# Three more tiles of the first batch in 16-bit pairs, and the work that turns weights into such pairs moved ahead of them

## The chip, the cores and the metric

The kernel runs on one core of one Trainium2 chip. The metric is the device time of one execution in microseconds (us); less is better. Besides TensorE (PE) the core has VectorE (DVE), ScalarE (ACT), GpSimd (POOL) and SyncE (SP), whose queue issues nearly all of the DMAs here.

## What is computed

Attention over channels, followed by a feed-forward layer on its result, in float32:

```python
qn = q / (np.linalg.norm(q, axis=1, keepdims=True) + 1e-06)      # q, k, v: (4, 6080, 256)
kn = k / (np.linalg.norm(k, axis=1, keepdims=True) + 1e-06)
s = kn.transpose(0, 2, 1) @ qn / tau                             # (4, 256, 256)
a = np.exp(s - s.max(-1, keepdims=True)); a /= a.sum(-1, keepdims=True) + 1e-09
x = (v @ a).reshape(24320, 256)
h = x @ w_in                                                     # 256 -> 2048
out = np.maximum(0.01 * h, h) @ w_out                            # 2048 -> 256
```

## The kernel before

The attention matrix of a batch is folded into the weights: W' = a @ w_in, so each batch needs only h = v @ W' and the second product. Every factor is held as a pair, a high part and a rest, and a product is made of three matmuls (high x high, rest x high, high x rest, `PASSES`). A pair is either of type fp32r or of 16 bits. 16-bit pairs need scales that are powers of two, found from the largest value of W_in (`w_scale`), of W_out (`wo_scale`) and of each tile of V (`v_scale`).

The tokens of a batch are cut into NT = 6 tiles of two halves, each half 512 columns wide in the first four tiles and 496 in the last two; tiles are counted here from 0 over the four batches, so tiles 0 to 5 are batch 0. The 2048 inner columns go in 8 pairs of blocks. One pair of one tile is a *window*; window w = 8 x tile + pair, 192 in all. `T16` is the first tile with 16-bit pairs: 6 before, that is all of batches 1 to 3.

A window of TensorE's list holds seven products (`block_product`, L811, 21 matmuls, a Strassen-like scheme) and, between them, the second product of the window before (`ffn_out`, L867, 24 matmuls). The seven products are collected through PSUM banks x and z. ACT copies bank x out (L847), DVE adds bank z to that (`add`, L841): add(h11), add(h22) and add(h12), in the order in which they come in a window. Bank z is used again only when its add is over, so a product that goes to z waits for DVE. From the sums, `leaky` makes pairs of the activated values: ACT the activation (L824), DVE the rest (L834, called g_split after what it writes).

All other work stands in slots between these: `slot` takes entries from a list for ACT, DVE or PE while their planned lengths fit the room of the slot (`put`, `put_steps`), and `at(w, ...)` enters work at the start of window w. The engines run their lists in this order. Such work is: the scores of the next batch (squares of q and k, added up on DVE, L223), sums of blocks of W_in for the products (`sums_work`, L999 to L1015), pairs of V (`v_split`, L762 to L773; `v_go` in 16 bits, `v_work` in fp32r), W_out's turning into 16-bit pairs (`wo_half`: DVE add L678, ACT, DVE L681, store), and copies of the output (`o_sb`) at the end of a tile.

A scale goes through four steps: `see` reduces a piece (DVE, L141), `gather` reduces these to one value per partition (L146) and stores it as a line in DRAM (0.5 KB, L147); `read`, a window later, fetches the line back into all partitions (64 KB into the tile `zeros`, L153); `find` makes the scale from it with five small DVE operations (L157 to L166), for V one more (L729). Before the change gather and find of a scale stand two windows or more apart.

## Time and profile before

| | |
|---|---|
| median of 3 runs | 2086.32 us (2085.83 to 2086.34) |
| the profiled execution | 2086.27 us, its span in the trace 2084.20 us |
| TensorE (PE) busy | 2076.7 us, 100% of the span, 9656 matmuls |
| VectorE (DVE) busy | 1600.7 us, 77%, 2905 instructions |
| ScalarE (ACT) busy | 1429.9 us, 69%, 2571 instructions |
| TensorE waiting for DVE's add before a product to bank z | 1.4 us in all, 3 times |

TensorE is occupied from end to end and granted its full clock throughout. The time is therefore the length of TensorE's list, and every wait that enters it. DVE and ACT have idle time on the average; how much there is in one window, and in which part of it, is seen only in the timeline.

### The profile page before, as it was taken

The numbers are of one execution on the slowest core, as the hardware profiler recorded it, in microseconds if no ns is written. First come the engines' busy times: TensorE is split into PE (matmuls) and PEld (weight loads), VectorE is DVE, ScalarE is ACT, GpSimd is POOL, SyncE is SP. The second block draws the span as 40 slices with busy tenths as digits, with TensorE's granted clock in tenths as the row PEclk, the third lists the DMA queues.
The fourth block names the chain that finished last, engine by engine and source line by source line (L and its number), as shares of the span: only waits on it lengthen the run. The fifth ranks groups of instructions, "written<-read, shape, count | busy, mean of one in ns | idle before, by whom it ended". The sixth has DMA issues, their size and how long they took to land.

```text
...
## 1 busy us (share of the span) xinstructions
PE 2076.7 (100%) x9656; PEld 1213.5 (58%) x9656; DVE 1600.7 (77%) x2905; ACT 1429.9 (69%) x2571; POOL 3.3 (0%) x11
## 2 busy tenths in 40 slices
...
GB/s 361 397 167 206 201 244 212 171 180 180 185 136 130 106 104 99 104 105 96 175 111 131 115 106 117 104 106 75 120 154 106 83 84 75 66 86 73 66 73 29
DMA packets 120168, 283.47 MB, mean 136 GB/s; under 512 B 15072, under 2 KB 40160, under 8 KB 120032
## 3 DMA queue, kind: packets, MB, share of 16 engines
...
HBM read 227.93 MB, written 53.75 MB: 135 GB/s over the span
## 4 chain that ended last, share of the span: by engine, by line
PE 98%; DVE 1%; DMA 1%; ACT 0%; issue 0%; SPq 0%; ACTq 0%; DVEq 0%
PE ps_o L867 48%; PE ps_x L811 24%; PE ps_z L811 16%; PE ps_s L253 3%; PE ps_y L811 2%; PE ps_y L253 2%; PE ps_s L1060 1%; PE ps_o L253 1%; DMA qk_raw<-in_k_dram 1%; PE ps_y L558 0%; PE ps_y L1060 0%; DVE sq_acc L210 0%; PE ps_z L558 0%; SPq L201 0%; ACT sq L209 0%
## 5 line engine op out<-in xcount | busy, mean ns | idle before, releaser
L867 PE MATMUL ps_o<-g_split,w_out_split 128*128 128x512 f16 (+3 forms) x4608 | 1123.3, 380 | 0.0
L834 DVE TENSOR_TENSOR g_split<-g,g_split 128x512 f16<-128x512 f32 (+3 forms) x768 | 525.0, 684 | 208.3 <-ACT g_split L824 201.1
L811 PE MATMUL ps_x<-v_split,w_split 128*128 128x512 f16 (+3 forms) x2280 | 620.3, 381 | 0.1
L867 PEld LDWEIGHTS <-w_out_split 128*128 128x128 f16 x3456 | 338.2, 98 | 400.0
L824 ACT ACTIVATE g<-h 128x512 f32<-128x512 f32 (+1 forms) x576 | 360.4, 626 | 281.7 <-DVE h L841 279.0
L841 DVE TENSOR_TENSOR h<-ps_z,h 128x512 f32<-128x512 f32 (+1 forms) x520 | 354.7, 682 | 234.0 <-ACT h L847 225.9
L847 ACT COPY h<-ps_x 128x512 f32<-128x512 f32 (+1 forms) x576 | 331.5, 575 | 292.8 <-PE ps_x L811 291.6
L811 PEld LDWEIGHTS <-w_split 128*128 128x128 f16 x3024 | 288.8, 98 | 342.2 <-issue 11.9
L811 PE MATMUL ps_z<-v_split,w_split 128*128 128x512 f16 (+3 forms) x1560 | 423.0, 380 | 1.4 <-DVE h L841 1.4
L824 ACT ACTIVATE g_split<-h 128x512 f16<-128x512 f32 (+3 forms) x576 | 351.4, 610 | 0.0
L867 PEld LDWEIGHTS ps_o<-g_split,w_out_split 128*128 128x128 f32 x1152 | 216.4, 188 | 43.5
L830 ACT CAST g_split<-g 128x512 f16<-128x512 f32 (+3 forms) x192 | 118.0, 615 | 5.9
L811 PEld LDWEIGHTS ps_x<-v_split,w_split 128*128 128x128 f32 x576 | 107.7, 188 | 22.4 <-ACT h L847 0.4
L824 ACT ACTIVATE g<-ps_x 128x512 f32<-128x512 f32 (+1 forms) x192 | 113.1, 589 | 9.7 <-PE ps_x L811 7.4
L764 DVE SCALAR_TENSOR_TENSOR v_split<-v_raw,v_scale,v_split 128x512 f16<-128x512 f32 (+1 forms) x125 | 93.2, 745 | 4.4
L223 DVE TENSOR_TENSOR sq_acc<-sq_acc,sq 128x512 f32<-128x512 f32 x141 | 96.3, 683 | 0.2
L220 ACT ACTIVATE sq<-qk_raw 128x512 f32<-128x512 f32 x141 | 87.5, 630 | 0.0
L811 PEld LDWEIGHTS ps_z<-v_split,w_split 128*128 128x128 f32 x408 | 76.2, 188 | 16.7 <-DVE h L841 1.4
L253 PE MATMUL ps_s<-qk_split 128*128 128x512 f32 x192 | 73.2, 391 | 0.0
L232 DVE TENSOR_TENSOR qk_split<-qk_raw,qk_split 128x512 fp32r<-128x512 f32 x96 | 65.6, 683 | 0.0
L785 DVE TENSOR_TENSOR v_raw<-v_raw 128x512 f32<-128x512 f32 (+1 forms) x94 | 64.0, 681 | 1.4
L253 PE MATMUL ps_y<-qk_split 128*128 128x512 f32 x192 | 60.3, 336 | 0.0
...
## 6 DMA issues: line engine op xcount, KB each, us to landing
w_split<-w_dram SPq DMA_DIRECT2D x144, 448.0 KB, 3.8
...
```

What stands on the lines that cost most here:

```text
L220: return nc.scalar.activation(out=out, in_=self.chunk(j), func=AF.Square)
L223: return nc.vector.tensor_tensor(out=self.acc[0], in0=self.acc[0], in1=sq, op=ALU.add)
L232: return nc.vector.tensor_tensor(out=sp[:, :, 1, :], in0=self.chunk(j), in1=f32(sp[:, :, 0, :]), op=ALU.subtract)
L253: mm = nc.tensor.matmul(out=out, lhsT=lhsT, rhs=rhs, start=start, stop=stop, skip_group_check=True)
L764: return nc.vector.scalar_tensor_tensor(out=sp[:, 1, 0:w], in0=src, scalar=up, in1=sp[:, 0, 0:w], op0=ALU.mult, op1=ALU.subtract)
L811: mm = nc.tensor.matmul(out=ps[:, 0:n], lhsT=w[:, x, a, :], rhs=sp[:, y, 0:n], start=first and k == 0, stop=k == 2, skip_group_check=True,)
L824: return nc.scalar.activation(out=to, in_=h[:, 0:n], func=AF.Prelu, alpha=0.01, scale=G_SCALE if i >= T16 else 1.0)
L830: issued["act"] = nc.scalar.copy(out=sp[:, 0, 0:n], in_=out[:, 0:n])
L834: issued["dve"] = nc.vector.tensor_tensor(out=sp[:, 1, 0:n], in0=out[:, 0:n], in1=f32(sp[:, 0, 0:n]), op=ALU.subtract)
L841: issued["dve"] = nc.vector.tensor_tensor(out=h[:, 0:n], in0=ps[:, 0:n], in1=h[:, 0:n], op=ALU.add)
L847: issued["act"] = nc.scalar.copy(out=h[:, 0:n], in_=ps[:, 0:n])
L867: issued["pe"] = nc.tensor.matmul(out=o_ps[i][j][h][:, 0:n], lhsT=wo_lhsT(i, x, f, h), rhs=sp[:, y, 0:n], start=p == 0 and early and k == ...
```

## The change

`T16` becomes 3, so tiles 3, 4 and 5 of batch 0 (w24 to w47) use 16-bit pairs too. All that these need is moved ahead of them:

- `w16_work(p)` in window 16 + p turns W' of one pair into 16 bits: at the window's start two DVE adds of 128x448 (high + rest), then in slots ACT, DVE, ACT, DVE, and a store of 448 KB. Tiles 3 to 5 load that (448 KB a window instead of 896).
- `wo_half`, eight times, now runs from w13 on (before: w24 to w34), and the loads of the result (`wo_load`) come in tile 2 instead of tile 5.
- The scales of W_in and W_out are found from sums that ACT accumulates (`summed`: squares for W_in, absolute values for W_out) instead of 16 DVE reduces. `gather` has one more small operation and `find(True)` five more (`roots`). W_in's gather is put in at w7 and its find at w9, W_out's at w10 and w12.
- Tiles 3 to 5 get their pairs of V by `v_scale_work` and `v_go`: gather, read, find, and then the 16-bit pair.
- The squares of batch 1 begin at w10 instead of w8, their loads are held back, the sums of W_in (`sums_work`) are chained one behind the other.
- `slot` no longer takes the list in its order, but by the window by which an entry is wanted (`wanted`, `due`).

The diff, cut to what the sections below speak of:

```diff
-    T16 = NT
+    T16 = 3
...
         def gather(self):
             last = nc.vector.tensor_reduce(out=self.top, in_=self.most, axis=AX.X, op=ALU.max)
+            last = nc.vector.tensor_scalar(
+                out=self.top, in0=self.top, scalar1=2.0**126, scalar2=None, op0=ALU.min
+            )
             nc.sync.dma_start(out=self.line, in_=self.top)
             at(now[0] + 1, self.read)
             return last
 
         def read(self):
...
+    def w16_work(p):
+
+        w, n = w_split[T16 - 1, p], NS * P // 2
+        o = work.tile([P, 2, NS * P], F16, name="w16", tag="qk_split", bufs=3)
+        t = [temp(name="w_whole")[:, 0:n] for _ in range(2)]
+        hi, lo = (f32(w[:, x].rearrange("p s f -> p (s f)")) for x in range(2))
+        xs = [slice(x * n, (x + 1) * n) for x in range(2)]
+        for x in range(2):
+            run("dve", lambda: nc.vector.tensor_tensor(out=t[x], in0=hi[:, xs[x]], in1=lo[:, xs[x]], op=ALU.add))
+
+        def high(x):
+            return nc.scalar.activation(out=o[:, 0, xs[x]], in_=t[x], func=AF.Copy, scale=w_scale.up)
+
+        def low(x):
+            ins = nc.vector.scalar_tensor_tensor(
+                out=o[:, 1, xs[x]], in0=t[x], scalar=w_scale.up, in1=o[:, 0, xs[x]], op0=ALU.mult, op1=ALU.subtract
+            )
+            if x:
+                nc.sync.dma_start(
+                    out=w16_dram[p].rearrange("p x f -> p (x f)"), in_=o.rearrange("p x f -> p (x f)")
+                )
+                w16_done[p] = now[0]
+            return ins
+
+        put_steps([
+            ("act", 0.6, lambda: high(0)), ("dve", 0.7, lambda: low(0)),
+            ("act", 0.6, lambda: high(1)), ("dve", 0.7, lambda: low(1)),
...
+        w, src = w_tile(i), w_dram[i // NT, p]
+        if T16 <= i < NT:
+            assert p in w16_done
+            src = w16_dram[p]
+        nc.sync.dma_start(out=f32(w.rearrange("p x s f -> p (x s f)")), in_=src.rearrange("p x f -> p (x f)"))
         w_split[i, p] = w
...
     def slot(queue, room):
         engine = queue.split("_")[0]
-        while todo[queue] and todo[queue][0][0] <= room and todo[queue][0][1].ready():
-            length, fn = todo[queue].popleft()
+        while True:
+            order = sorted(range(len(todo[queue])), key=lambda n: todo[queue][n][1].due or now[0] + 3)
+            for n in order:
+                length, fn = todo[queue][n]
+                if fn.ready() and (length <= room or fn.due is None):
+                    break
+            else:
+                return
+            if length > room:
+                return
+            del todo[queue][n]
             room -= length
             with in_order(engine):
...
             else:
-                at(w + 1, v_scale_work, i + 1)
-                at(w + 3, v_go, i + 1, 3)
-                at(w + 4, v_go, i + 1, 3)
-                at(w + 5, v_go, i + 1, 3)
-                at(w + 6, v_go, i + 1, 3)
+                with wanted(w + 2 if i < NT - 1 else None):
+                    at(w + 1, v_scale_work, i + 1)
+                with wanted(w + 6 if i < NT - 1 else None):
+                    for x in (3, 4, 5, 6):
...
-        begin_at, span = (NPAIR, 20) if b == 1 else (0, 28)
+        begin_at, span = (NPAIR + 2, 19) if b == 1 else (0, 28)
         when = {j: w0 + begin_at + j * span // NCHUNK for j in range(NCHUNK)}
         for i in range(len(sc.groups)):
-            at(max(w0 - 2, when[i * G] - (1 if b == 1 else 3)), lambda sc=sc, i=i: sc.load(i, qk_raw()))
+            if b == 1:
+                at(when[i * G] - 1, raw_wanted.append, (sc, i))
+            else:
+                at(max(w0 - 2, when[i * G] - 3), lambda sc=sc, i=i: sc.load(i, qk_raw()))
...
+    def wo_go(n):
+        if n < wo_n:
+            with wanted(TL + n - 3):
+                put_steps([*wo_half(n), ("call", wo_go, n + 1)], True)
+
+    TL = (T16 - 1) * NPAIR
+    with wanted(NPAIR + 2):
+        for n in range(wo_n):
+            at(NPAIR + n // 4, put, "act", 0.65, lambda n=n: summed(
+                f32(wo_region(n)), wo_scale.most[:, n:n + 1], AF.Abs
+            ))
+    at(NPAIR - 1, put, "dve", 0.2, w_scale.gather)
+    at(NPAIR + 1, put, "dve", 1.2, lambda: w_scale.find(True), (), True)
+    at(NPAIR + 2, put, "dve", 0.2, wo_scale.gather)
+    at(NPAIR + 4, put, "dve", 0.6, wo_scale.find, [("dve", 0.3, weights_down), ("call", wo_go, 0)], True)
+    for p in range(NPAIR):
+        with wanted(TL + p):
+            at(TL + p, w16_work, p)
```

`order`'s rows show where this puts work on DVE. L901, L908 and L251 are the lines of L834, L841 and L223 after the change; a name ahead of `<-` is what a row writes, and `[waits ...]` are the semaphores that it waits for (DMAHW is a DMA).

**W_in's scale, w8 and w9.** On DVE, before, from add(h11) of w9 (h_1810) over add(h22) (h_1851) to add(h12):

```order
L841 TENSOR_TENSOR h_1810<-ps_z_1805,h_1810 128x512 [waits PE_49,Activation_49]
L223 TENSOR_TENSOR sq_acc_1695<-sq_acc_1695,sq_1815 128x512 [waits DVE_49,Activation_49]
L834 TENSOR_TENSOR g_split_1829<-g_1828,g_split_1829 128x512 [waits Activation_49]
L841 TENSOR_TENSOR h_1851<-ps_z_1806,h_1851 128x512 [waits DMAHW0_49,Activation_49]
L223 TENSOR_TENSOR sq_acc_1695<-sq_acc_1695,sq_1838 128x512 [waits DVE_49]
L834 TENSOR_TENSOR g_split_1864<-g_1863,g_split_1864 128x512 [waits PE_49,Activation_49]
L841 TENSOR_TENSOR h_1836<-ps_z_1806,h_1836 128x512 [waits PE_49]
```

The same place after the change, from the row behind add(h11) on; L165 to L176 are the find, and h_1880 is add(h22):

```order
L165 TENSOR_REDUCE w_scale_134<-zeros_72 128x1 [waits DMAHW6_49]
L184 TENSOR_SCALAR w_scale_134<-w_scale_134 128x1 [waits DVE_49]
L187 TENSOR_SCALAR w_scale_134<-w_scale_134 128x1 [waits DVE_49]
L190 TENSOR_SCALAR w_scale_134<-w_scale_134 128x1 [waits DVE_49]
L191 TENSOR_SCALAR w_scale_134<-w_scale_134 128x1 [waits DVE_49]
L192 ISA w_scale_134<-w_scale_134 128x2 [waits DVE_49]
L168 TENSOR_SCALAR w_scale_134<-w_scale_134 128x1 [waits DVE_49]
L169 TENSOR_SCALAR w_scale_134<-w_scale_134 128x1 [waits DVE_49]
L172 TENSOR_SCALAR w_scale_134<-w_scale_134 128x1 [waits DVE_49]
L176 TENSOR_SCALAR w_scale_134<-w_scale_134 128x1
L901 TENSOR_TENSOR g_split_1856<-g_1855,g_split_1856 128x512 [waits Activation_49]
L908 TENSOR_TENSOR h_1880<-ps_z_1824,h_1880 128x512 [waits DMAHW0_49,Activation_49]
```

The gather of this scale (L148, L149) stands in w8 right behind add(h11) and one v_split step. The ten rows of find, with a wait for the read, came between add(h11) and the pair that follows it; two additions of squares went.

**V's scale for tile 4, w26 and w27.** On DVE, before, from add(h11) of w27 (h_3617) to its add(h22):

```order
L841 TENSOR_TENSOR h_3617<-ps_z_3612,h_3617 128x512 [waits PE_49,Activation_49]
L223 TENSOR_TENSOR sq_acc_1695<-sq_acc_1695,sq_3549 128x512 [waits DVE_49]
L834 TENSOR_TENSOR g_split_3632<-g_3631,g_split_3632 128x512 [waits Activation_49]
L681 SCALAR_TENSOR_TENSOR wo16_3423<-wo_whole_3422,wo_scale_128,wo16_3423 128x512
L223 TENSOR_TENSOR sq_acc_1695<-sq_acc_1695,sq_3595 128x512 [waits DVE_49]
L1006 TENSOR_TENSOR win_s_3526<-win_s_3526,win_s_3113 128x512
L841 TENSOR_TENSOR h_3659<-ps_z_3613,h_3659 128x512 [waits Activation_49]
```

After the change, in w26 from the last reduce of the scale to add(h22), with its gather (L148, L149):

```order
L143 TENSOR_REDUCE v_scale_3544<-v_raw_3391 128x1
L148 TENSOR_REDUCE v_scale_3544<-v_scale_3544 128x1 [waits DVE_49]
L149 TENSOR_SCALAR v_scale_3544<-v_scale_3544 128x1 [waits DVE_49]
L1106 TENSOR_TENSOR win_t_3438<-win_s_2358,win_t_3438 128x512
L908 TENSOR_TENSOR h_3678<-ps_z_3625,h_3678 128x512 [waits Activation_49]
```

and in w27 from the row behind add(h11) to add(h22) (h_3786):

```order
L251 TENSOR_TENSOR sq_acc_1923<-sq_acc_1923,sq_3739 128x512 [waits DVE_49,Activation_49]
L1097 TENSOR_TENSOR win_s_2360<-win_s_2360,win_s_2358 128x512
L901 TENSOR_TENSOR g_split_3750<-g_3749,g_split_3750 128x512 [waits Activation_49]
L165 TENSOR_REDUCE v_scale_3544<-zeros_72 128x1 [waits DMAHW5_49]
L168 TENSOR_SCALAR v_scale_3544<-v_scale_3544 128x1 [waits DVE_49]
L169 TENSOR_SCALAR v_scale_3544<-v_scale_3544 128x1 [waits DVE_49]
L172 TENSOR_SCALAR v_scale_3544<-v_scale_3544 128x1 [waits DVE_49]
L176 TENSOR_SCALAR v_scale_3544<-v_scale_3544 128x1
L796 TENSOR_SCALAR v_scale_3544<-v_scale_3544,rest_down_146 128x1 [waits DVE_49]
L829 TENSOR_SCALAR v_split_3760<-v_raw_3391,v_scale_3544 128x496
L831 SCALAR_TENSOR_TENSOR v_split_3760<-v_raw_3391,v_scale_3544,v_split_3760 128x496 [waits DVE_49]
L908 TENSOR_TENSOR h_3786<-ps_z_3730,h_3786 128x512 [waits Activation_49]
```

The find (L165 to L176 and L796) and the first half step of v_split (L829, L831) came ahead of add(h22), one window behind the gather; before, the pair of V needed no scale and conversions of W_out stood here.

**The start of a window of tile 2 (w18).** On DVE, before, from the last but one pair of w17 to the add(h11) of w18 (h_2706) and the v_split step behind it:

```order
L834 TENSOR_TENSOR g_split_2680<-g_2679,g_split_2680 128x512 [waits Activation_49]
L834 TENSOR_TENSOR g_split_2685<-g_2684,g_split_2685 128x512 [waits Activation_49]
L841 TENSOR_TENSOR h_2706<-ps_z_2701,h_2706 128x512 [waits PE_49,Activation_49]
L769 CAST v_split_2714<-v_raw_2482 128x512 [waits DMAHW2_49]
L773 TENSOR_TENSOR v_split_2714<-v_raw_2482,v_split_2714 128x512 [waits DVE_49]
```

After the change, at the start of w18, whose add(h11) is h_2763:

```order
L901 TENSOR_TENSOR g_split_2732<-g_2731,g_split_2732 128x512 [waits Activation_49]
L251 TENSOR_TENSOR sq_acc_1923<-sq_acc_1923,sq_2736 128x512 [waits DVE_49,Activation_49]
L901 TENSOR_TENSOR g_split_2740<-g_2739,g_split_2740 128x512 [waits Activation_49]
L595 TENSOR_TENSOR w_whole_2753<-w_split_2428 128x448
L595 TENSOR_TENSOR w_whole_2754<-w_split_2428 128x448
L908 TENSOR_TENSOR h_2763<-ps_z_2758,h_2763 128x512 [waits DMAHW4_49,PE_49,Activation_49]
L251 TENSOR_TENSOR sq_acc_1923<-sq_acc_1923,sq_2768 128x512 [waits DVE_49,Activation_49]
```

The two adds of W' (L595) came between the last pair of the window before and add(h11).

## Rows read from the trace of the kernel before

**Rows 1.** The page: busy time and instructions by engine; the chain that ended last.
```profile
PE 2076.7 (100%) x9656; PEld 1213.5 (58%) x9656; DVE 1600.7 (77%) x2905; ACT 1429.9 (69%) x2571; POOL 3.3 (0%) x11
...
PE 98%; DVE 1%; DMA 1%; ACT 0%; issue 0%; SPq 0%; ACTq 0%; DVEq 0%
```

**Rows 2.** Timeline of PE, one fp32r window (w20): start, us, operation, count.
```profile
301.43 0.84 PE L811 MATMUL ps_x<-v_split,w_split 128*128 128x512 f32 x3
...
304.60 0.84 PE L811 MATMUL ps_z<-v_split,w_split 128*128 128x512 f32 x3
...
309.59 0.84 PE L811 MATMUL ps_z<-v_split,w_split 128*128 128x512 f32 x3
...
311.63 0.84 PE L811 MATMUL ps_x<-v_split,w_split 128*128 128x512 f32 x3
```

**Rows 3.** Timeline of PE, one 16-bit window (tile 19): first products of two windows.
```profile
1700.91 0.81 PE L811 MATMUL ps_x<-v_split,w_split 128*128 128x512 f16 x3
...
1710.62 0.81 PE L811 MATMUL ps_x<-v_split,w_split 128*128 128x512 f16 x3
```

**Rows 4.** Tiles by stretch: length; PE, PEld, DVE, ACT, POOL; PEclk, DMA share, GB/s.
```profile
260.60:342.20 81.60, 81.60 (x361) 67.54 (x360) 71.89 (x117) 62.83 (x113) 0.00 (x0) 1.00 0.64 220
...
425.30:510.90 85.60, 85.60 (x387) 71.76 (x387) 66.04 (x129) 55.57 (x102) 0.00 (x0) 1.00 0.51 171
510.90:596.10 85.20, 85.20 (x383) 71.46 (x382) 67.00 (x135) 51.97 (x95) 0.00 (x0) 1.00 0.58 192
...
942.30:1024.60 82.30, 81.66 (x390) 39.61 (x389) 62.67 (x125) 53.56 (x102) 0.00 (x0) 1.00 0.39 124
1024.60:1104.90 80.30, 80.30 (x382) 38.63 (x381) 67.08 (x140) 50.80 (x96) 0.00 (x0) 1.00 0.46 146
```

**Rows 5.** Timeline of DVE in w80: add(h22).
```profile
950.63 0.66 DVE L841 TENSOR_TENSOR h<-ps_z,h 128x496 f32<-128x496 f32 x1
```

**Rows 6.** Timeline of PE in w80: the product behind that add [idle time, releaser].
```profile
951.35 0.79 PE L811 MATMUL ps_z<-v_split,w_split 128*128 128x496 f16 x3 [0.60 <-DVE h L841]
```

**Rows 7.** Timeline of DVE, tile 2: around add(h11) in w17, add(h11) in w22.
```profile
272.50 0.68 DVE L834 TENSOR_TENSOR g_split<-g,g_split 128x512 fp32r<-128x512 f32 x1
273.10 0.68 DVE L841 TENSOR_TENSOR h<-ps_z,h 128x512 f32<-128x512 f32 x1
...
323.46 0.69 DVE L841 TENSOR_TENSOR h<-ps_z,h 128x512 f32<-128x512 f32 x1 [0.18 <-PE ps_z L811]
```

**Rows 8.** DMA issues by line: KB each and median us from issue to landing.
```profile
v_scale_line<-v_scale SPq DMA_DIRECT2D x18, 0.5 KB, 7.5
...
w_scale_line<-w_scale SPq DMA_DIRECT2D x1, 0.5 KB, 9.9
```

**Rows 9.** Tiles v_scale_line (stores and reads) and zeros (reads): landing times.
```profile
DMA to landing us min/median/max: 4.4/6.6/8.2
...
DMA to landing us min/median/max: 4.4/5.4/6.2
```

**Rows 10.** Timeline of DVE in w8: the v_split step behind add(h11).
```profile
181.90 0.68 DVE L773 TENSOR_TENSOR v_split<-v_raw,v_split 128x512 fp32r<-128x512 f32 x1
```

**Rows 11.** Timeline of DVE in w41, v_scale's find: first, last, and the v_split behind.
```profile
546.64 0.28 DVE L157 TENSOR_REDUCE v_scale<-zeros 128x1 f32<-128x128 f32 x1
...
547.57 0.21 DVE L729 TENSOR_SCALAR v_scale<-v_scale,rest_down 128x1 f32<-128x1 f32 x1
...
549.10 0.48 DVE L762 TENSOR_SCALAR v_split<-v_raw,v_scale 128x512 f16<-128x512 f32 x1
```

**Rows 12.** Timeline of SP's DMA queue in w8.
```profile
182.60 0.81 SPq L750 DMA_DIRECT2D v_raw<-in_vT_dram  x2
```

**Rows 13.** Timeline of PE: the first product of w9.
```profile
189.21 0.84 PE L811 MATMUL ps_x<-v_split,w_split 128*128 128x512 f32 x3
```

**Rows 14.** DVE groups by form: SCALAR_TENSOR_TENSOR to 16 bits, 256 and 512 columns.
```profile
L602 DVE SCALAR_TENSOR_TENSOR w_rest<-w_s,w_scale,w_rest 128x256 f16<-128x256 f32 x48 | 21.0, 478 | 0.0
...
L681 DVE SCALAR_TENSOR_TENSOR wo<-wo_whole,wo_scale,wo 128x512 f16<-128x512 f32 x8 | 6.0, 745 | 0.0
```

141 lines of the change are left out of this document (92 added, 49 removed).

## The prediction

> **What bounds the kernel now.** I read the page's busy shares and chain first, then busy time by tile, then the timelines of single windows (a window is one pair of one tile; w = 8 x tile + pair, tiles counted from 0, so the change's tiles 4 to 6 are numbers 3 to 5, w24 to w47). TensorE is busy all the time: the chain that ended last is 98% PE, while DVE has 77% of the span and ACT 69% [rows 1]. So a change pays only where it shortens TensorE's own list, and costs only where it makes TensorE wait, which it hardly does now.
>
> How long TensorE takes depends on the pair's type. An fp32r window starts at 301.43 and the next at 311.63: 10.20 us [rows 2]. A 16-bit window of the same 45 matmuls takes 9.71 (1700.91 to 1710.62) [rows 3]. The 496-wide tiles of batch 0 (tiles 4 and 5, from 425.3 and 510.9) take 85.6 and 85.2; their counterparts in batch 1 (tiles 10 and 11, from 942.3 and 1024.6), already 16-bit with the same extra matmuls, 82.3 and 80.3 [rows 4].
>
> The second thing to see is how tight the other engines' dates are. The products of a window that go through bank z start 3.17 us (304.60) and 8.16 us (309.59) after its first matmul [rows 2]; each needs a DVE add that empties the bank (add(h11) and add(h22)). Where that add is late, TensorE waits at once: in w80 an o_sb copy stands ahead of add(h22), the add ends at 950.63 + 0.66 = 951.29, and the product starts at 951.35, after 0.60 of idling [rows 5, 6]. So an add has to end 0.05 us before its product: at +3.12 and +8.11 in an fp32r window, and at +7.7 for the second one in a 16-bit window (8.16 x 9.71 / 10.20, less 0.05). Now add(h11) of an ordinary tile-2 window is over at +2.3 (w22 begins at 321.83; 323.46 + 0.69), 0.8 us early [rows 7].
>
> **What the change gives.** Tile 3: eight windows by 10.20 - 9.71 = 3.9 us (a half window is lost at its start, where the second product still has the tile before's fp32r pairs, and another won in w48). Tiles 4 and 5: 85.6 + 85.2 - 82.3 - 80.3 = 8.2 us [rows 4]; w80's stall is in the 82.3, and w32 of the changed kernel has the same order. TensorE's instruction counts do not change. Together **-12.1 us**, if TensorE never waits.
>
> **What it costs.** Four kinds of work come to other engines; three meet TensorE's dates.
>
> *A, the scale of W_in.* A scale is found by a gather on DVE, a 0.5 KB store, a 64 KB broadcast read and a find on DVE. The store takes 7.5 (v_scale) to 9.9 us (w_scale) to land, the read 5.4, from 4.4 to 6.2 in 20 of them [rows 8, 9]. Now find stands two windows behind the gather and waits for nothing. In the change the gather is in w8 behind the v_split that ends at 181.90 + 0.68 = 182.58, so over at 182.9 (two ops of at most 0.2) [rows 10, 11]; its store queues behind SP's two 512 KB loads (182.60, 0.81 long) and goes at 183.4 [rows 12]. Data: 183.4 + 8.7 (half way between 7.5 and 9.9) + 5.4 = 197.5. Find stands second in w9, which begins at 189.21 [rows 13], ahead of add(h22): it would start at +8.3, when add(h22) should be over. Behind the data come ten small ops (the six now from 546.64 to 547.57 + 0.21 = 1.1 [rows 11]; five of them without the last one 0.9, and five more for the roots: 1.8), one g_split start to start (0.60) and the add (0.68), so it ends at 8.3 + 3.1 = 11.4 against 8.1: **+3.3**. Bounds: store 7.5 and read 4.4 give 183.4 + 11.9 + 3.1 - 189.2 - 8.1 = 1.1; 9.9 and 6.2 give 5.3.
>
> *B, the scale of tile 4's V.* In w26 the gather comes behind add(h11) (ends +2.3), two square sums, a g_split, and one reduce: 2.3 + 4 x 0.62 + 0.3 = +5.1. With 0.2 to the issue, 7.5 and 5.4 the data are there at w26 + 18.2, which is w27 + 8.5, since w26 is 9.71 long. In w27 find's six ops (1.1), the first half of v_split (0.48 [rows 11] and an STT of 0.745 [rows 14], about 1.1 from start to start) and the add (0.68) come behind it: add(h22) ends at 11.4 against 7.7, **+3.7**. Bounds: 2.6 with a read of 4.4, 5.3 with 8.2 and 6.2, the longest V scale transfers [rows 9]. The same pair for tile 3 (w18 to w20) and tile 5 (w33 to w35) is two windows apart and costs nothing, as now; the wo scale (w10 to w13) too.
>
> *C, tile 2.* W' of tile 3 to 5 is turned into 16-bit pairs in w16 to w23: per window two adds and two STT on DVE of 128x448. 512 columns take 0.69 and 0.745, 256 STT columns 0.478 [rows 7, 14]; by that slope 448 take about 0.62 and 0.68, and start to start 0.54 and 0.60, since an instruction that does not need the one before starts 0.08 before its end (272.50 and 273.10, each 0.68 long [rows 7]). The two adds stand right ahead of add(h11): 1.08 of the 0.8 us that it has. Then it is over at about +3.1 in the ordinary window, on the date to 0.05: between 0 and 0.25 us late in each, and 0.5 where DVE came late out of the window before; I take 1.7 in all. In w17, whose start holds the o_sb copies, add(h11) ends at 273.78 now, w17 + 3.0 (260.6 + 10.2 = 270.8 [rows 4, 7]), and then at 4.1: +1.0. In all, DVE's list of tile 2 (from 260.6) is now 117 instructions [rows 4], 77 us by their lengths, 69 start to start. By the order the change adds 14 adds, 14 STT, 9 wo conversion steps, 8 v_split and 4 reduce steps and some small ones of V's scale (34 us of lengths), and takes 9 reduces, 9 win sums, 12 v_split steps and 2 square sums away (20): 91 by lengths, 81 start to start, in 81.6 us of TensorE [rows 4]. It is uneven: counted by the same prices, w20 and w21 hold 11.3 and 10.7 for 10.20, so 1.6 more. C: **+4.3**; bounds 1.0 (w17 alone, all else covered) and 7.
>
> *The rest costs nothing.* ACT gets 16 casts and 16 accumulating passes, about 8 us in tile 2, whose 62.8 busy of 81.6 [rows 4] hide them; without that cover each late copy would cost what a DVE add does. SP gets eight 448 KB stores in tile 2, where DMA is at 0.64 of its time [rows 4]; W' reloads for tiles 3 to 5 are halved. The 16 reduces that go are on DVE, which is not the bound where they stood.
>
> Sum: -12.1 + 3.3 + 3.7 + 4.3 = -0.8. The profiled execution took 2086.27 for a span of 2084.20, and the median of the runs is 2086.32, so 2085.5: no change that 0.2% (4.2 us, about what a measurement of this kernel can tell) would show.
>
> **The rivals.** *The waits are mostly covered (faster).* If the round trips are at their short end (A 1.1, B 2.6) and DVE's overlap leaves only w17's late add (C 1.0), the sum is -12.1 + 4.7 = -7.4: 2078.9; with nothing waiting at all 2074.2. For it: the short ends do occur, and 0.05 us in one add per window decides six windows of C. Against: both landings are medians over 18 transfers [rows 8], and w8's store goes behind two large loads. The Trainium skill, page "DMA: Bandwidth & Descriptors", section "Anatomy of one DMA", puts the fixed cost of a transfer (there one of GpSimd's queue) near 2.0 us: by that page the round trip would be about 4 us as an estimate, A and B would vanish and the time be 2085.5 - 7.0 = 2078.5. The rows (7.5 and 5.4) do not agree with it in this kernel, so it gets no weight beyond the short end's.
>
> *DVE becomes the bound of tile 2 (slower).* If the 0.08 us of overlap is not had by instructions that wait for ACT or a DMA, the list counts by its lengths: 91 for 81.6 us, so C is 9.4, and -12.1 + 7.0 + 9.4 = +4.3, 2090.6; with tile 3 (about 81 of lengths in 79) 2092. It decides once C passes 9.3, that is when nearly nothing of 117 overlaps is left. For it: nearly every added instruction waits on another engine. Against it: 272.50 to 273.10 holds for a g_split that waits for ACT. On a page: the Trainium skill, "VectorE: DVE Perf Modes", section "The DRAIN you can't avoid", says that the next op does not start until the pipe is empty, and by it lengths add up in full; the trace disagrees with the 0.60 between starts of 0.68 [rows 7].
>
> That the 16-bit windows are not shorter in batch 0 I give no weight: 144 windows already run so.
>
> **How the numbers follow.** Forecast (waits of 8 to 16 us, 2082.1 to 2090.5): 0.60. Waits covered, below 2082.1: 0.28. DVE the bound, or both round trips at their long ends (5.3 + 5.3 + 5.5 = +4.0 net) above 2090.5: 0.12. These are also same, faster and slower. Range 2079 to 2091: it leaves out about 0.1 of the first rival (below its own sum) and 0.1 of the second.
>
> **What would show it.** In the changed profile: 16-bit windows of 9.71 and 9.41 in w24 to w47; one stall of TensorE on add(h22) of 3.3 in w9 with DVE's find waiting for the zeros read, and one of 3.7 in w27; tile 2 at 85.9 instead of 81.6, w17, w20 and w21 longest. I am wrong if find does not wait (round trip under 10 us), if tile 2 stays under 83, or if tile 3 to 5 do not come down.

## The result, and the profile after

| | before | after |
|---|---|---|
| median | 2086.33 us (2085.83 to 2086.84) | 2106.94 us (2105.91 to 2110.58, 4 runs) |
| ratio, 95% interval | | 1.0102 [1.0084, 1.0119] |
| profiled execution, span | 2086.27, 2084.2 us | 2105.91, 2104.1 us |

The changed kernel is slower by 20.6 us, outside the range of 2079 to 2091. The page of the changed kernel, busy time by engine and the chain that ended last (before: [rows 1]):

```profile
PE 2075.0 (99%) x9656; PEld 1116.9 (53%) x9656; DVE 1621.2 (77%) x2982; ACT 1442.2 (69%) x2619; POOL 3.3 (0%) x11
...
PE 91%; DMA 3%; DVE 3%; ACT 3%; issue 1%; SPq 0%; DVEq 0%; ACTq 0%
```

TensorE is busy for 1.7 us less than before, but the chain is no longer its own: DMA, DVE and ACT hold 9% of it. The same by tiles 1 to 5 (stretch, length, then busy time of PE, PEld, DVE, ACT, POOL; PEclk, DMA share, GB/s):

```profile
179.20:272.80 93.60, 85.64 (x362) 69.14 (x361) 66.61 (x123) 66.47 (x128) 0.00 (x0) 0.96 0.48 173
272.80:365.90 93.10, 85.50 (x362) 66.14 (x361) 83.01 (x143) 67.94 (x126) 0.00 (x0) 1.00 0.61 199
365.90:453.00 87.10, 81.39 (x369) 38.36 (x369) 75.18 (x142) 61.91 (x115) 0.52 (x1) 0.96 0.65 178
453.00:535.40 82.40, 81.77 (x391) 39.64 (x390) 67.91 (x135) 55.63 (x106) 0.00 (x0) 1.00 0.50 162
535.40:615.70 80.30, 80.30 (x383) 38.57 (x382) 67.25 (x141) 50.89 (x95) 0.00 (x0) 1.00 0.49 146
```

Tiles 4 and 5 took 85.6 and 85.2 before [rows 4] and now take what their counterparts in batch 1 take. Tile 2 took 81.6 and takes 93.1. Tile 1, for which 3.3 more were forecast, took 11.4 more, and tile 3 lost in one window twice what it gained in the others. Here and below the length of a window is the distance of its first product from that of the next window, read from PE's timeline as in [rows 2, 3]; the two of w9, for instance, are 189.99 and 208.28. All these lengths and waits are read from one profiled execution of each kernel. Four places make the loss:

| place | before | after | difference |
|---|---|---|---|
| w9 | 10.20 | 18.29 | +8.1 |
| w12 | 10.20 | 13.33 | +3.1 |
| tile 2 (w16 to w23) | 81.6 | 93.1 | +11.5 |
| w27 | 10.20 | 17.32 | +7.6 over 9.71, the 16-bit window's length |
| tile 3 without that, tiles 4 and 5 | 253.8 | 242.2 | -11.6 |
| all else | | | +1.2 |

**w9**, four engines of the timeline: SP's queue, ACT's copy of bank x, DVE's find and add(h22), and the product that waits (start, us, operation; in brackets idle time before it and who ended it):

```profile
184.27 0.38 SPq L152 DMA_DIRECT2D w_scale_line<-w_scale  x1
193.43 0.33 SPq L160 DMA_DIRECT2D zeros<-w_scale_line  x1
...
194.32 3.80 SPq L961 DMA_DIRECT2D out_dram<-o_sb  x4
...
202.36 0.58 ACT L914 COPY h<-ps_x 128x512 f32<-128x512 f32 x1 [6.05 <-DMA out_dram<-o_sb]
...
199.50 0.28 DVE L165 TENSOR_REDUCE w_scale<-zeros 128x1 f32<-128x128 f32 x1 [6.08 <-DMA zeros<-w_scale_line]
...
202.98 0.69 DVE L908 TENSOR_TENSOR h<-ps_z,h 128x512 f32<-128x512 f32 x1 [1.03 <-ACT h L914]
...
203.00 1.65 PE L878 MATMUL ps_x<-v_split,w_split 128*128 128x512 f32 x3 [4.93 <-ACT h L914]
```

There are two waits side by side. DVE's find waits 6.1 us for its data, as step A said. But TensorE waits for ACT: the copy needs a buffer that an o_sb tile still holds (ACT's copies `h`, the o_sb tiles, the scratch that ACT's sums write to and the halves of W' and W_out take turns in one ring of nine buffers), and the store of that tile left late, because the read of the scale's line stood at the head of SP's queue until its line had landed (184.27 to 193.4, 9.1 us). The four stores behind it went at 194.3 to 198.1.

The same place in one-microsecond slices (columns as above):

```profile
200.00:201.00 1.00, 0.00 (x0) 0.00 (x0) 0.82 (x6) 0.00 (x0) 0.00 (x0) 1.00 0.97 393
201.00:202.00 1.00, 0.00 (x0) 0.00 (x0) 0.92 (x4) 0.00 (x0) 0.00 (x0) 0.84 1.02 392
202.00:203.00 1.00, 0.00 (x0) 0.00 (x1) 0.02 (x1) 0.58 (x1) 0.00 (x0) 0.50 0.89 340
...
207.00:208.00 1.00, 1.00 (x4) 0.80 (x3) 0.38 (x2) 0.84 (x2) 0.00 (x0) 0.50 0.64 158
208.00:209.00 1.00, 1.00 (x5) 0.82 (x4) 0.56 (x1) 0.00 (x0) 0.00 (x0) 0.75 1.03 430
209.00:210.00 1.00, 1.00 (x6) 0.80 (x5) 0.00 (x0) 0.72 (x2) 0.00 (x0) 1.00 0.67 280
```

TensorE has stood since 198.1. In the slice from 201 its granted clock falls to 0.50, the lower of its two levels (1.2 GHz), and stays there until the slice from 208. So w9 loses 4.9 us of its 8.1 by standing and 2.6 by the restart at the lower clock: from 203.00 to the window's end at 208.28 it takes 5.28 us for what a plain window does in 2.72. The other 0.6 us are short waits ahead of the long one.

**w12.** SP's queue and ACT:

```profile
213.99 0.33 SPq L152 DMA_DIRECT2D wo_scale_line<-wo_scale  x1
221.63 0.33 SPq L160 DMA_DIRECT2D zeros<-wo_scale_line  x1
...
224.06 1.36 SPq L229 DMA_DIRECT2D qk_raw<-in_q_dram  x1
...
226.72 0.42 SPq L229 DMA_DIRECT2D qk_raw<-in_k_dram  x1
...
234.57 0.63 ACT L248 ACTIVATE sq<-qk_raw 128x512 f32<-128x512 f32 x1 [4.28 <-DMA qk_raw<-in_k_dram]
```

Four q and k loads go in one bunch behind the read of W_out's line and two W_in loads; ACT's square of that data waits, and its next copy of bank x stands behind the square (TensorE idle 2.79 us).

**w27.** SP's store and read of tile 4's V scale, DVE's find and add(h22), the product behind it:

```profile
392.43 0.38 SPq L152 DMA_DIRECT2D v_scale_line<-v_scale  x1
...
401.96 0.32 SPq L160 DMA_DIRECT2D zeros<-v_scale_line  x1
...
406.69 0.29 DVE L165 TENSOR_REDUCE v_scale<-zeros 128x1 f32<-128x128 f32 x1 [6.12 <-DMA zeros<-v_scale_line]
...
408.92 0.69 DVE L908 TENSOR_TENSOR h<-ps_z,h 128x512 f32<-128x512 f32 x1
...
409.66 1.44 PE L878 MATMUL ps_z<-v_split,w_split 128*128 128x512 f16 x3 [5.66 <-DVE h L908]
```

This is step B's chain, longer: w27 begins at 396.06, the find at +10.6 (forecast +8.5), and the restart is again at the lower clock (0.50 in the slices from 408 to 412).

**Tile 2.** Groups of DVE and then of PE by line (busy us, mean ns, idle us before them and who ended it):

```profile
L901 DVE TENSOR_TENSOR g_split<-g,g_split 128x512 fp32r<-128x512 f32 x33 | 22.7, 689 | 3.5 <-ACT g_split L891 3.3
L908 DVE TENSOR_TENSOR h<-ps_z,h 128x512 f32<-128x512 f32 x24 | 16.4, 685 | 5.2 <-ACT h L914 5.1
L251 DVE TENSOR_TENSOR sq_acc<-sq_acc,sq 128x512 f32<-128x512 f32 x17 | 11.6, 685 | 0.1
L595 DVE TENSOR_TENSOR w_whole<-w_split 128x448 f32<-128x448 f32 x16 | 9.3, 620 | 0.9 <-DMA wo_dram<-wo 0.9
L601 DVE SCALAR_TENSOR_TENSOR w<-w_whole,w_scale,w 128x448 f16<-128x448 f32 x13 | 8.6, 678 | 0.0
...
L878 PE MATMUL ps_x<-v_split,w_split 128*128 128x512 f32 (+1 forms) x97 | 27.9, 394 | 1.8 <-ACT h L914 1.8
L878 PE MATMUL ps_z<-v_split,w_split 128*128 128x512 f32 x72 | 21.5, 407 | 5.8 <-DVE h L908 5.6
```

DVE is occupied 83.0 us (before 71.9, [rows 4]), which alone is more than the 81.6 us that TensorE needs, and TensorE waits for its adds in nearly every window: 5.6 us for DVE and 1.8 for ACT. The other 4 us show as busy time (85.5 us for the work of 81.6, at a granted clock of 1.00). The place is the product to bank z behind add(h11), the one of the first add in a window. In w17, which begins at 283.06:

```profile
283.06 0.84 PE L878 MATMUL ps_x<-v_split,w_split 128*128 128x512 f32 x3
...
285.69 0.96 PE L878 MATMUL ps_x<-v_split,w_split 128*128 128x512 f32 x3
...
287.62 0.96 PE L878 MATMUL ps_z<-v_split,w_split 128*128 128x512 f32 x3 [0.96 <-DVE h L908]
```

It starts 4.56 us into the window where a plain one has 3.17 [rows 2], 1.4 us late, of which the profile shows 0.96 as idle, and it takes 0.96 us instead of 0.84. In w17 to w23 this product is 0.3 to 2.0 us late, 7.0 in all.

### The profile page after: what moved, and what is told of

Same layout as the page of the kernel before. It is cut to its first block, busy times and chain, and to the rows that moved or that the text cites. A ratio compares the mean times of both kernels' runs of the same rounds, so it can differ in the third digit from the quotient of the medians.

```text
span 2104.1 us, 27456 instructions
## 1 busy us (share of the span) xinstructions
PE 2075.0 (99%) x9656; PEld 1116.9 (53%) x9656; DVE 1621.2 (77%) x2982; ACT 1442.2 (69%) x2619; POOL 3.3 (0%) x11
## 4 chain that ended last, share of the span: by engine, by line
PE 91%; DMA 3%; DVE 3%; ACT 3%; issue 1%; SPq 0%; DVEq 0%; ACTq 0%
PE ps_o L934 43%; PE ps_x L878 22%; PE ps_z L878 15%; PE ps_s L281 4%; PE ps_o L281 2%; PE ps_y L878 2%; PE ps_y L281 2%; PE ps_s L1154 1%; DMA out_dram<-o_sb 1%; ACT g L891 1%; DVE h L908 1%; DMA qk_raw<-in_k_dram 1%; ACT g_split L891 1%; DMA v_scale_line<-v_scale 0%; DMA w_scale_line<-w_scale 0%
## 5 line engine op out<-in xcount | busy, mean ns | idle before, releaser
L934 PE MATMUL ps_o<-g_split,w_out_split 128*128 128x512 f16 (+2 forms) x4608 | 1118.9, 379 | 0.0
L901 DVE TENSOR_TENSOR g_split<-g,g_split 128x512 f16<-128x512 f32 (+2 forms) x768 | 524.9, 684 | 209.4 <-ACT g_split L891 201.9
L934 PEld LDWEIGHTS <-w_out_split 128*128 128x128 f16 x4032 | 394.6, 98 | 466.6 <-issue 1.7
L878 PE MATMUL ps_x<-v_split,w_split 128*128 128x512 f16 (+2 forms) x2280 | 618.7, 380 | 9.7 <-ACT h L914 9.5
L908 DVE TENSOR_TENSOR h<-ps_z,h 128x512 f32<-128x512 f32 (+1 forms) x520 | 354.3, 681 | 211.5 <-ACT h L914 204.8
L878 PE MATMUL ps_z<-v_split,w_split 128*128 128x512 f16 (+2 forms) x1560 | 423.2, 380 | 13.5 <-DVE h L908 13.3
L891 ACT ACTIVATE g_split<-h 128x512 f16<-128x512 f32 (+2 forms) x576 | 351.2, 610 | 0.0
L897 ACT CAST g_split<-g 128x512 f16<-128x512 f32 (+2 forms) x192 | 117.9, 614 | 5.9
L934 PEld LDWEIGHTS ps_o<-g_split,w_out_split 128*128 128x128 f32 x576 | 109.0, 189 | 23.9 <-issue 0.5
L831 DVE SCALAR_TENSOR_TENSOR v_split<-v_raw,v_scale,v_split 128x512 f16<-128x512 f32 (+1 forms) x146 | 108.7, 745 | 5.2
L251 DVE TENSOR_TENSOR sq_acc<-sq_acc,sq 128x512 f32<-128x512 f32 x141 | 96.4, 684 | 4.7 <-ACT sq L248 4.1
L829 DVE TENSOR_SCALAR v_split<-v_raw,v_scale 128x512 f16<-128x512 f32 (+1 forms) x146 | 69.5, 476 | 0.0
L878 PEld LDWEIGHTS ps_x<-v_split,w_split 128*128 128x128 f32 x288 | 53.9, 190 | 24.1 <-ACT h L914 13.0
```

Source lines behind the costliest of these rows:

```text
L251: return nc.vector.tensor_tensor(out=self.acc[0], in0=self.acc[0], in1=sq, op=ALU.add)
L829: nc.vector.tensor_scalar(out=sp[:, 0, 0:w], in0=src, scalar1=up, scalar2=None, op0=ALU.mult)
L831: return nc.vector.scalar_tensor_tensor(out=sp[:, 1, 0:w], in0=src, scalar=up, in1=sp[:, 0, 0:w], op0=ALU.mult, op1=ALU.subtract)
L878: mm = nc.tensor.matmul(out=ps[:, 0:n], lhsT=w[:, x, a, :], rhs=sp[:, y, 0:n], start=first and k == 0, stop=k == 2, skip_group_check=True,)
L891: return nc.scalar.activation(out=to, in_=h[:, 0:n], func=AF.Prelu, alpha=0.01, scale=G_SCALE if i >= T16 else 1.0)
L897: issued["act"] = nc.scalar.copy(out=sp[:, 0, 0:n], in_=out[:, 0:n])
```

## The experiments

**Two theories for w9.** Late find: DVE's find ahead of add(h22) holds TensorE, as step A has it. Queue: what holds it is SP's queue behind the waiting read. The first two kernels move the one and the other. (In all kernels but the one with the queue alone, a V scale's `gather` is put in by the last reduce ahead of it.) First the finds of W_in's scale and of tile 4's V scale, each a window later:

```diff
-                    for x in (3, 4, 5, 6):
-                        at(w + x, v_go, i + 1, 3)
+                    for x, n in ((4, 6), (5, 3), (6, 3)) if i == 3 else ((3, 3), (4, 3), (5, 3), (6, 3)):
+                        at(w + x, v_go, i + 1, n)
...
-    at(NPAIR + 1, put, "dve", 1.2, lambda: w_scale.find(True), (), True)
+    at(NPAIR + 2, put, "dve", 1.2, lambda: w_scale.find(True), (), True)
```

> Only the two early finds move: W_in's scale is found in w10 instead of w9, V's scale for tile 4 in w28 instead of w27. The order of the DMA queue up to the read of W_in's scale is as in the changed kernel. If TensorE stood in w9 and w27 because DVE waited in find (the find theory), both windows come down to their plain 10.2 and 9.7 us: 2106.9 - 8.1 - 7.6 = about 2091 us. If in w9 it stood because the read of the scale, waiting at the head of SP's queue for its line, held back the stores of o_sb, and ACT's copy out of bank x got its buffer only when these had landed (the queue theory), w27 goes to 9.7, but w9 keeps nearly all of its 18.3 us: about 2099 us.

Measured 2107.50 us, 1.010 [1.0085, 1.0115], as long as the changed kernel and above what either theory gave (2091, 2099). w27 falls to 9.71: there the find was the cause. w9 stays at 18.10 though nothing waits on DVE, and ACT's copy shows why:

```profile
201.29 0.58 ACT L914 COPY h<-ps_x 128x512 f32<-128x512 f32 x1 [5.91 <-DMA out_dram<-o_sb]
```

So the late find alone does not make w9. What w27 gave was lost at w12 (16.46; the W_out line went later, the loads behind it too) and in w42 (14.28), where a step of the next batch's W' waits 4.6 us for what the step before it stored.

The read behind the stores, on top of these edits: the read of W_in's line is put a window later and issued behind the last o_sb store, the find in w11, W_out's gather too.

```diff
+            with ExitStack() as stack:
+                if self is w_scale:
+                    stack.enter_context(tc.issue_after(out_last[0].ins))
+                nc.sync.dma_start(out=self.all, in_=self.line.rearrange("p o -> (p o)").partition_broadcast(P))
...
-    at(NPAIR + 2, put, "dve", 0.2, wo_scale.gather)
+    at(NPAIR + 3, put, "dve", 0.2, wo_scale.gather)
```

> As the run before, and the read of W_in's scale is put behind the four stores of o_sb in SP's queue (find in w11, W_out's gather in w11 too). Queue theory: w9 goes to about 10.2 us as well, about 2091 us; w12 or w13, behind the read of W_out's scale, still stands for some 3 us. Find theory: nothing more than in the run with the later finds alone, since there DVE did not wait any more.

Measured 2099.64, 1.0063 [1.0048, 1.0078], 8.6 us above the queue theory's 2091. w9 14.53, w12 10.20. The stores now go at 189.45 and the copy still waits 3.09 us for them. In return tile 2 grew to 96.1, w20 to 16.06, where one of the additions ahead of add(h11) (L595 of the changed kernel) waits for the store of a W_out half: both take buffers of the ring of nine.

**Tile 2.** No additions: the 16-bit pairs are made of W's high parts alone. This leaves the low parts of W' out in tiles 3 to 5.

```diff
-        t = [temp(name="w_whole")[:, 0:n] for _ in range(2)]
-        for x in range(2):
-            run("dve", lambda: nc.vector.tensor_tensor(out=t[x], in0=hi[:, xs[x]], in1=lo[:, xs[x]], op=ALU.add))
+        t = [hi[:, xs[x]] for x in range(2)]
```

> The changed kernel without the two DVE adds of 128x448 at the start of each window of tile 2; the 16-bit pairs of W' are made from the high parts alone, so the low parts of W' are left out in tiles 3 to 5. Tile 2 takes 93.1 us in the changed kernel instead of 81.6. If the adds' place ahead of add(h11), and the fullness of DVE, make that, tile 2 falls to 82 to 84 us and the whole to about 2097. If instead buffers that wait for stores to land (the ACT copy in w17, the second add in w20) make it, w17 keeps its wait of 1.4 us for the ACT copy and tile 2 stays over 85: about 2100.

Measured 2093.78, 1.0037 [1.0022, 1.0051], below the 2097 of the first theory, since w27 came to 13.63 as well (its find waited 4.2 us and not 6.1, and the granted clock stayed at 1.00), for which the edit gives no reason. The tile from 272.3, as above:

```profile
272.30:356.40 84.10, 83.44 (x362) 66.29 (x361) 74.98 (x127) 68.25 (x126) 0.00 (x0) 1.00 0.65 214
```

DVE has 8.0 us less to do and the tile is 9.1 us shorter, at the upper end of the 82 to 84 expected. The product behind add(h11) starts 3.17 to 3.39 us into every window. So 9.1 of tile 2's 11.5 us hang on these additions and the buffers that they take.

Half of the conversion in tile 1 instead (pairs 4 to 7 from tile 1's W'), with the edits of the kernel with the read behind the stores, the find of tile 3's scale later and the loads of W' for tile 6 two windows later:

```diff
-        w, n = w_split[T16 - 1, p], NS * P // 2
+        w, n = w_split[T16 - (2 if p in (4, 5, 6, 7) else 1), p], NS * P // 2
```

> The read behind the stores and the finds two windows behind the gathers, and W' of pairs 4 to 7 turned into 16 bits in tile 1 (w12 to w15) instead of tile 2. Queue theory with a full DVE in tile 2: w9 and w27 without loss (-15.7), tile 2 near 85 with some of its loss moved to tile 1, w12 unsettled: 2106.9 - 15.7 - 6 = 2080 to 2086 us. If the loss in tile 2 comes from the 16-bit work itself wherever it stands, tiles 1 and 2 together keep their 11 us and the time is about 2091.

Measured 2117.52, 1.0148 [1.0133, 1.0163], where the theories gave 2080 to 2086 and 2091: a miss. w17 took 18.80, with a 7.0 us wait of the copy for an o_sb store, and w19 17.73, with ACT waiting 5.8 us for a W_out store; w24 and w27 took 15.20 and 15.47. Fewer additions in tile 2 didn't free it (100.5): both waits in it are for buffers of the ring of nine.

**Queue and find apart.** First the queue alone: the reads of all scale lines are issued by GpSimd, the find stays.

```diff
-            nc.sync.dma_start(out=self.all, in_=self.line.rearrange("p o -> (p o)").partition_broadcast(P))
+            nc.gpsimd.dma_start(out=self.all, in_=self.line.rearrange("p o -> (p o)").partition_broadcast(P))
```

> One edit: the read of each scale line back from DRAM is issued from GpSimd's queue in place of SyncE's; nothing else of the changed kernel is touched, and no find is put later. Theory (a read that waits at the head of SyncE's in-order queue holds back everything queued behind it): the four o_sb stores of w8 leave before 192 us in place of 194.3, ScalarE's copy in w9 no longer comes 6.1 us late; w12 falls from 13.3 to about 10.2, since the q and k loads no longer stand behind the read of W_out's line. VectorE's find in w9 still waits for its line (6.1 us), and so does the one in w27 (17.3 us as before), so w9 comes down by 0 to 5 us only. Sum: -3.1 at w12, -0 to -5 at w9: 2099 to 2104. Rival (the stores themselves land late for another reason, contention of the loads with the stores, and the queue's order doesn't matter): w12 stays at 13.3 and the time stays at 2107 within 1.5.

Measured 2101.37, 1.0074 [1.0059, 1.0089], inside the theory's 2099 to 2104. Copy, stores and find in w9:

```profile
189.99 2.78 SPq L961 DMA_DIRECT2D out_dram<-o_sb  x4
...
199.04 0.59 ACT L914 COPY h<-ps_x 128x512 f32<-128x512 f32 x1 [2.87 <-DMA out_dram<-o_sb]
...
199.68 0.29 DVE L165 TENSOR_REDUCE w_scale<-zeros 128x1 f32<-128x128 f32 x1 [6.41 <-DMA zeros<-w_scale_line]
```

The copy comes 3.2 us earlier in the window, and now the find ends last. w9 16.39, w12 11.13 (10.2 expected); w27, where only the find waits, 18.20.

Queue and find together, the edits of the first kernel and of this one:

> The first experiment's edits (the find of W_in's scale one window later, the find of tile 4's V scale two windows after its gather) and the reads of the scale lines on GpSimd's queue. Theory (two waits in w9, VectorE's for the line and ScalarE's for a buffer whose store is held behind the read): against the first experiment (2107.5) w9 falls from 18.1 to 10 to 12, w12 from 16.5 to 10.2, w42 from 14.3 to about 11; 2091 with 3 to spare either way; what is left over the kernel before is tile 2. Rival (late stores for a reason that isn't SyncE's queue): w9 and w12 stay, 2105 to 2109.

Measured 2093.76, 1.0036 [1.0024, 1.0048]: w42 10.84 as expected, w9 12.33 just above its 10 to 12, w12 13.01 not (10.2 expected). The third holder, the ring: the scratch of the sums from another ring.

```diff
-        unread = temp(name="unread").bitcast(F16)[:, 0:values.shape[-1]]
+        unread = work.tile([P, TW], F32, name="g", bufs=3).bitcast(F16)[:, 0:values.shape[-1]]
```

> The run before it, and the scratch that takes the unread output of ScalarE's sums comes from the ring of the LeakyReLU tiles (3 buffers) in place of the ring of nine that ScalarE's h copies, the o_sb tiles and the halves of W' share. Theory (what is left in w9 is the ring of nine: a copy needs a buffer whose o_sb store hasn't landed): the waits of ScalarE's copy for o_sb stores in w9 and w17 shrink or go, 2087 to 2090, 2 to 4 us below the run before it. Rival (the ring isn't what is left): the same as the run before it, within 1 us.

Measured 2090.74, 1.0021 [1.0012, 1.0031]: w9 10.28, so its loss is gone, and w12 14.85, which gave 1.8 us back, for a clock that fell behind a wait of 2.72 us there (last section): 0.7 above the theory's range. Five kernels, w9 by what they free, and how long TensorE stands idle in it:

| find moved | queue free | ring freed | w9 | idle |
|---|---|---|---|---|
| no | no | no | 18.29 | 4.93 |
| yes | no | no | 18.10 | 4.74 |
| no | yes | no | 16.39 | 3.87 |
| yes | yes | no | 12.33 | 1.29 |
| yes | yes | yes | 10.28 | 0 |

Either of the first two alone saves 0.2 or 1.9 us, both together 6.0, the ring another 2.0. In idle time the same steps are 0.2, 1.1, 3.6 and 1.3: in the first three kernels the granted clock fell to 0.50 behind the wait, in the last two it did not, so that part of what the pair saves is the clock.

**W' in place.** No sum: VectorE forms scale x high - (16-bit high), then adds scale x low to that; slots of tiles 2 and 5 0.7 us wider, tile 3's find in w20, the loads of W' for tile 6 two windows later.

```diff
+        def part(x):
+            return nc.vector.scalar_tensor_tensor(
+                out=o[:, 1, xs[x]], in0=hi[:, xs[x]], scalar=w_scale.up, in1=o[:, 0, xs[x]], op0=ALU.mult, op1=ALU.subtract
+            )
...
-                out=o[:, 1, xs[x]], in0=t[x], scalar=w_scale.up, in1=o[:, 0, xs[x]], op0=ALU.mult, op1=ALU.subtract
+                out=o[:, 1, xs[x]], in0=lo[:, xs[x]], scalar=w_scale.up, in1=o[:, 1, xs[x]], op0=ALU.mult, op1=ALU.add
```

> The run before it, the finds of tile 3's V scale also two windows after its gather, and tile 2's W' made without the sum in float32: VectorE forms scale*hi-high and then adds scale*lo to it in place, in slots behind add(h11) and add(h22), so that no addition stands ahead of add(h11) and no buffer of the ring of nine is taken; tile 2's slots of VectorE are 0.7 us wider for it, and tile 5's as well. VectorE's work in a window of tile 2 grows by about 0.2 us (two more scalar_tensor_tensor, two additions less). Theory (tile 2 loses by the additions ahead of add(h11) and by the ring): tile 2 at 83 to 85 us in place of 93, the time 2078 to 2082, below the kernel before. Rival (VectorE's load as such is what bounds tile 2): tile 2 at 89 or more, the time 2085 to 2088.

Measured 2090.66, 1.0021 [1.0012, 1.0030]. Tile 2 came to 86.5 (from 91.8), between theory and rival. The time missed the range by w12 (14.11) and by tiles 4 to 9, together 3.1 us longer (512.8 after 509.7): in w42 a step of W' waits 3.0 us for what its neighbour stored. First tile 5's slots and tile 3's find back as they were.

> The run before it (halves in place) without two of its edits: tile 5's slots of VectorE back at the changed kernel's width, and the find of tile 3's V scale back in its place. Theory (the run before it won in tile 2 and lost again in tile 5, where wider slots put a step that reads what its neighbour had just stored into one window, and in the row of tiles behind it): tile 5 at 80 to 82 in place of 86.4, tiles 7 and 8 1.4 us less each, tiles 4 and 6 some 5 us more; tile 2 at 86 to 88; w12 still 13 to 14. 2087 to 2089. Rival (tile 5's loss has nothing to do with the slots): 2090 to 2091.

2092.79, 1.0031 [1.0020, 1.0042]: tile 5 80.9 as expected, but with the change's own entries for tile 3's find that find came in w19 and waited for its line: w19 16.14, tile 2 92.1, and the time above both ranges. W_in's find and W_out's gather a window later still:

```diff
-    at(NPAIR + 2, put, "dve", 1.2, lambda: w_scale.find(True), (), True)
-    at(NPAIR + 2, put, "dve", 0.2, wo_scale.gather)
+    at(NPAIR + 3, put, "dve", 1.2, lambda: w_scale.find(True), (), True)
+    at(NPAIR + 3, put, "dve", 0.2, wo_scale.gather)
```

> The run before it, with the find of W_in's scale and the gather of W_out's moved to the window after the next (w11). In SyncE's list the four q and k loads of w10 and w11, which stood in a bunch behind two W_in loads, come apart again as they were in the kernel before. Theory (w12 waits for the bunch: four loads queued within 2 us land together 8 to 9 us later): w12 falls from 14 to about 10.3, nothing else of tile 1 changes; 2083 to 2086, unless tile 5's steps stall as much again (up to 3 us). Rival (w12 is lost by VectorE's own load): w12 stays above 13, 2087 to 2089.

2090.42, 1.0018 [1.0009, 1.0027]. The q loads leave SP at 204.1, 211.6, 220.8 and 224.4, where the kernel with the other ring had 204.7 and then 215.1 and 216.3 together, behind two W_in loads; w12 is 10.20 and tile 1 82.2 (before 82.15). So w12 was the bunch: with the reads off SP's queue the bunch was still there (w12 11.13, 13.01 and 14.85 in the three kernels of the table). The time is above the 2083 to 2086, for w19 is still there, 16.43 (DVE's find, then the lower clock):

```profile
304.12 0.28 DVE L165 TENSOR_REDUCE v_scale<-zeros 128x1 f32<-128x128 f32 x1 [4.03 <-DMA zeros<-v_scale_line]
```

Tile 5's slots 0.3 us wider:

> The run before it, with tile 5's slots 0.3 us wider, so that a store of W' and the step that reads it stand a window apart. Expected 2082 to 2085, 1 to 4 us below the kernel before, by tile 4 and 5 at 161 to 163 us together (170.7 in the kernel before) and tile 2 at 86 (81.6 before). If tile 2's VectorE list is what stays, not below 2084; if w42 stalls, 2086 or more.

2090.90, 1.0022 [1.0013, 1.0031], no better: w19 17.06, and w42 13.03. A miss. In place alone, without queue and ring:

> The changed kernel with W' halves in place (no additions ahead of add(h11), no buffers of the ring of nine for them), tile 2's slots 0.7 us wider, the find of tile 4's V scale two windows after its gather, and the loads of W' for tile 6 two windows later; the reads stay on SyncE's queue, the find of W_in's scale and the scratch stay where the changed kernel has them. Theory (tile 2 loses by the additions and their buffers alone): tile 2 at 85 to 88 in place of 93.1, w27 at 9.7, w9 at 18 and w12 at 13 as in the changed kernel: 2107 less 5 to 8 less 7.6: 2091 to 2095. Rival (tile 2 needs the queue or the other ring as well): tile 2 at 91 or more, 2097 to 2100.

2099.26, 1.0062 [1.0048, 1.0076], inside the rival's 2097 to 2100; tile 2 is 90.7, just under the rival's 91, with w19 at 15.41 by the same find; w9 18.77 and w12 12.78 stay, w27 is at 9.71, w42 took 14.48. With w19 at the 10.75 of the first kernel in place, tile 2 would be 86.0, an estimate.

**Tile 3's find out of w19.** The kernel with the loads apart, and:

```diff
-                    for x, n in ((4, 6), (5, 3), (6, 3)) if i == 3 else ((3, 3), (4, 3), (5, 3), (6, 3)):
+                    for x, n in ((4, 6), (5, 3), (6, 3)) if i == 3 else ((4, 3), (5, 6), (6, 3)) if i == 2 else ((3, 3), (4, 3), (5, 3), (6, 3)):
...
-            slot("dve", 2.15 if i == T16 - 1 else 1.45 if i == NT - 1 else 1.45 if i else 2.8)
+            slot("dve", {2: 2.15, 3: 1.8, 4: 1.8}.get(i, 1.45) if i else 2.8)
```

> The run with the loads apart, and the find of tile 3's V scale one window later (w20 in place of w19); tile 3's and tile 4's slots of VectorE are 0.3 us wider so that the steps of W' still come in time. Theory (w19's 16.4 us is that find's wait, and what is left of tile 2 is VectorE's list): w19 at 10 to 11, tile 2 at 86 to 87, tile 1 at 82.2, tiles 3 to 5 together at 243 to 246 (253.8 before): 2083 to 2086, even with the kernel before or 3 us below it. Rival (tile 2 is held by something else): tile 2 at 90 or more, 2088 to 2091.

Measured **2082.18, 0.9979 [0.9970, 0.9988]**: less than both kernels, by 0.2% against the kernel before, and 0.8 us below the theory's range. (Both of DVE's slots in a window of tiles 3 and 4 are wider; the diff shows one.) Tiles 1 to 5, as above:

```profile
179.10:261.90 82.80, 82.37 (x362) 67.11 (x360) 64.63 (x120) 65.66 (x126) 1.21 (x2) 1.00 0.68 183
261.90:347.70 85.80, 84.52 (x361) 66.11 (x359) 81.75 (x139) 68.16 (x125) 0.53 (x1) 1.00 0.69 216
347.70:429.10 81.40, 80.29 (x369) 37.93 (x369) 76.36 (x145) 61.94 (x115) 1.07 (x2) 1.00 0.66 191
429.10:510.50 81.40, 81.40 (x391) 39.64 (x390) 69.40 (x136) 55.99 (x107) 0.53 (x1) 1.00 0.59 176
510.50:590.90 80.40, 80.40 (x382) 38.61 (x381) 66.01 (x137) 50.54 (x94) 0.53 (x1) 1.00 0.52 146
```

w19 10.77, tile 2 85.8. DVE is occupied 81.75 of these 85.8 us. That its list is what is left of C is argued, not shown: the idle time that the profile gives TensorE here is 0.7 us for ACT's copies and 0.2 for DVE's adds, and the kernel without additions, with DVE at 75.0 us, took 84.1 too.

> The same, with tile 3's and tile 4's slots another 0.35 us wider and tile 5's 0.3, so that W' for tile 6 is made in tiles 4 and 5 in another order, a window between a store and the step that reads it. Theory: tile 2 as in the run before it (86 to 87); tiles 3 to 5 within 2 us of it, lower if the store and the step no longer meet; 2082 to 2087. Rival (wider slots make VectorE the bound of tiles 3 and 4 as well): tiles 3 and 4 together at 165 or more (162 to 163 expected), 2087 to 2090.

2086.00, 0.9999 [0.9990, 1.0008], at the theory's upper end, but with the rival's sign: tiles 3 and 4 took 165.9 together (162.7 in the run before it). Tile 2 86.4, tile 5 82.6.

## Why the prediction was wrong

**The gain** of 12.1 was right: tiles 4 and 5 gave 8.1 (8.2 forecast), tile 3 without w27's excess 3.6 (3.9). The rest of the sum failed; against the forecast's -0.8 the span grew by 19.9:

| term | forecast | measured |
|---|---|---|
| gain of tiles 3 to 5 | -12.1 | -11.6 |
| A (w9) | +3.3 | +8.1 |
| W_out's scale (w12) | 0 | +3.1 |
| B (w27) | +3.7 | +7.6 |
| C (tile 2) | +4.3 | +11.5 |
| all else | 0 | +1.2 |

**A: the mechanism was there, and another one above it was missed.** The find came at w9 + 9.5 (199.50 - 189.99; +8.3 forecast), since the line took 9.1 us to land and not 8.7, and the read 6.0 and not 5.4. But TensorE waited for ACT. The step that failed is where the prediction looked at SP only for how long the store queues: it named what stands behind find on DVE, and not what stands behind the read on SP. The read waits for its line at the head of a queue that works in order, 9.1 us, and behind it stood the o_sb stores that free ACT's buffers. The Trainium skill, page "DMA: Bandwidth & Descriptors", section "Anatomy of one DMA", states that DMA engines don't wait on semaphores; the issuing sequencer does, before it dispatches. The trace agrees: 193.43 for the read, 194.32 for the first store behind it. The table of w9 shows the find, the queue and the ring each to hold it in turn; 2.6 of the 8.1 us are the lower clock behind the wait, which no term held.

**B: the right wait, mis-sized.** Idle was 5.7 us where 3.7 was forecast: the store left at w26 + 6.1 (+5.3 forecast), the line took 9.5 us to land (7.5 was taken, the median; 8.2 the bound), the read 4.7 (5.4 taken). Of the rest of the 7.6, 1.9 us, the lower clock behind the wait makes 1.8 (409.66 to 413.38 for what a plain window does in 1.94), which no term held. (Of the prediction's figures, A's upper bound adds up to 5.2 and not 5.3, and the read's landing is a median over 20 transfers, not 18 [rows 9]; the forecast doesn't change by it.) The find a window later makes w27 9.71: shown.

**"The wo scale costs nothing"** failed too: the find indeed waited for nothing, but four loads came in a bunch behind the read of the line, which held SP's queue from 214 to 221.6, and behind two W_in loads. That the bunch holds w12 is shown by 10.20 when the loads are apart. The read is at most a part of it: 13.33 fell to 11.13 with the read on GpSimd's queue, and in the next two kernels with it there w12 was 13.01 and 14.85. Why the loads bunch there stays open.

**C: the place was right, the size 2.7 times too small.** The step that failed is the lateness of add(h11). The prediction gave it 0 to 0.25 us in an ordinary window, 0.5 behind a late one and 1.0 in w17, 2.7 in all; in the trace the product behind it is 0.3 to 2.0 us late in each of w17 to w23, 7.0 in all, and without the additions it is on time to 0.2 and the tile takes 84.1. The length of DVE's list was counted well (81 us from start to start, 83.0 occupied), and w17, w20 and w21 are the longest, as forecast (13.4, 12.6 and 11.8 us). What was put at nothing is ACT, under "the rest costs nothing": DVE stood idle 10.1 of the tile's 93.1 us, 5.1 of it for ACT's copies and 3.3 for ACT's half of the pairs, while ACT itself waited 1.8 us for an o_sb store and 4.1 for DVE's steps of W' and W_out and V's scale. How much of the difference is the additions' place, how much their two buffers of the ring and how much ACT's lateness, no run separates. The kernel with the find out of w19 has tile 2 at 85.8, nearly the 85.9 of the forecast; that is chance, for it has no additions ahead of add(h11).

**The rivals.** Waits covered: nothing for it; the lines of 0.5 KB took 9.1, 7.6 and 9.5 us to land, so the short ends did not come. The 2.0 us of fixed cost of the page that the prediction named there (the Trainium skill, "DMA: Bandwidth & Descriptors", section "Anatomy of one DMA") are not seen here either. DVE the bound of tile 2: the side was right, and so was DVE's list being longer than TensorE's, but not its reason, that no instruction overlaps the next: 190.04 follows 189.44 by 0.60 for an operation of 0.68 at the start of w9 of the changed kernel as before [rows 7], and tile 2's instructions, about 92 us by their lengths, occupy 83.0. The section that the prediction named there (the Trainium skill, "VectorE: DVE Perf Modes", "The DRAIN you can't avoid") adds that a next operation that is not held starts earlier, so the 0.60 agrees with it. The rival's 2090.6 is also 16 us short. What was given for slower was DVE's list and the long ends of both round trips; SP's queue, the ring of nine and the clock behind a wait were in no rival.

Why a line of 0.5 KB takes 7.6 to 9.5 us to land stays open; that wasn't tried.
